# Attention plus gated MLP on one core: the second head pair is made the second unit of work, the tail the third, and the early loads are reordered

## The chip, the cores and the metric

The kernel runs on one core of a Trainium2 chip. The metric is device time in microseconds (us); the median of three runs of the kernel before is 283.36 us (282.83 to 284.4). The profiled execution has a span of 283.1 us. A difference of about 0.5% (1.4 us) is what a measurement of this kernel can tell from none.

## The reference

Two stages, for 8 batches, 8 heads, 576 tokens, head width 64, 128 features:

```python
def phi(x):
    proj = np.einsum('bhsd,df->bhsf', x, w_phi)
    proj = proj - np.max(np.abs(proj), axis=-1, keepdims=True)
    return np.concatenate([np.exp(proj), np.exp(-proj)], axis=-1)
q_p, k_p = (phi(q), phi(k))
kv = np.einsum('bhsf,bhsd->bhfd', k_p, v)
z = np.sum(k_p, axis=2)
num = np.einsum('bhsf,bhfd->bhsd', q_p, kv)
den = np.einsum('bhsf,bhf->bhs', q_p, z)[..., None] + 1e-06
x = (num / den)            # then (b, s, h*d)

h = np.maximum(x @ w_in, 0.0)
u, v = (h[..., :d_ff // 2], h[..., d_ff // 2:])
v_n = (v - mean(v)) / np.sqrt(var(v) + 1e-06)
v_s = np.einsum('ts,bsd->btd', w_spatial, v_n) + b_spatial[None, :, None]
out = (u * v_s) @ w_out
```

The first stage is linear attention with features exp(p) and exp(-p) of the projections p, scaled by their largest absolute value; the second is an MLP whose gate mixes tokens through `w_spatial`.

## The kernel before

**Units.** Of the 576 tokens of a batch, 512 are the main part (four blocks of 128) and 64 the tail. A *pair unit* is the main part of two heads of one batch (four per batch); a *tail unit* holds the tails of two batches, all heads. In the list `units`, the tail unit of a group of two batches stands ahead of that group, except for the first group, where it stands behind the first pair (lines 562 to 569). I call the four pairs of batch 0 p0 to p3. Before the change the order is p0, tail, p1, p2, p3, then the four pairs of batch 1, the next tail, batch 2 and so on.

**What a unit does.** `a_transpose` turns k and q (bf16 in SBUF) into kT and qT through TensorE and PSUM, with copies on VectorE. `a_keys` projects the keys (L256), takes the largest absolute value per token and head on VectorE (L268, `mk`), and the exponentials on ScalarE (L271, `kf`). `a_scale` computes the scale `em` on ScalarE (L291) and multiplies v with it on GpSimd (L296, `vs`; L298); for a tail unit `tail_scale` does this for one batch of the two (L311, `vst`; L313). `a_queries` takes the query maxima (L282) and splits them into two bf16 parts, `mhl`: on VectorE for the first five units, on GpSimd after that (L285, L286). `a_max_t` transposes `mhl` on TensorE (L317). `a_qfeat` makes the query features (L338 to L349, exponentials L355 on ScalarE). `a_kv` sums kf times vs, with the tail's part, over tokens (L368, L370); `a_num` multiplies by the query features and divides (L388); `a_x_t` transposes the result.

**The order of the work.** `step(i)` runs over the units as a software pipeline: in step i the keys and queries of unit i are done, the transposes of unit i+1 (`next`), and the later parts of earlier units by the lags in `LAGS`, `FIRST` and `FT`. Between them `fill` takes tasks of the MLP of a batch from a queue: `b_v` (L437), its ReLU (L439) and statistics (L440), `b_root` (L447 to L450 on GpSimd), `b_ln` (L454 on GpSimd, writes `vn`), `b_u` (L492), `b_s` (L513, reads `vn`), `b_o` (L538). Each engine takes its own instructions strictly in program order; what is wrapped in `pin` keeps its place, the rest may be moved by the framework's scheduler.

**Loads.** k and q are fp32 in memory and are cast to bf16 by the transfer itself; such transfers are issued by GpSimd (software queue, q0 in the profile). Transfers without a cast go through SyncE (hardware queue, q1). The loads of the head of the program: k and q of p0 as fp32 (`first`, cast on VectorE), v of batch 0 in one transfer of 1 MB and the tail's v through SyncE, and through GpSimd the tails of k and q, then k and q of p1, then of p2 and p3. The dictionary `io` holds what is issued behind a given step: the loads of batch 1 and all weights at steps 1 to 4, and the loads of batch b from 6 steps ahead of its first unit. `weights_with_max` builds `wm`, which the units from batch 2 on need: 12 GpSimd instructions (L230 to L232), not pinned.

Buffers that two groups use in turn, `vst` (two tiles, zeros) and `vnt` (two tiles), are filled by ScalarE at the start.

Of the kernel before, what the change touches and what calls it, by code (L numbers as in the profile page):

```python
# [8 lines left out]
FP32 = mybir.dt.float32  # L9
BF16 = mybir.dt.bfloat16  # L10
AF = mybir.ActivationFunctionType
ALU = mybir.AluOpType
# [4 lines left out]
def kernel(  # L17
# [15 lines left out]
    nc = tc.nc  # L33

    B, H, S, D = q.shape
    F = w_phi.shape[1]
    DM = moe_w_in.shape[0]
    DFF = moe_w_in.shape[1]
    HALF = DFF // 2
    P = 128  # L40
    KC = DM // P
    NP = H // 2
    NB = 4
    T0 = NB * P
# [3 lines left out]
    DA = D + 2  # L48

    cpool = ctx.enter_context(tc.tile_pool(name="const", bufs=1))  # L50
# [4 lines left out]
    s2 = ctx.enter_context(tc.tile_pool(name="stage_b", bufs=2))  # L55
# [4 lines left out]
    def pin(start):  # L60
        return lambda *a, **kw: tc.keep_in_program_order(start(*a, **kw))

    def main_ap(t, b, h0=0, n=H):
        return bass.AP(tensor=t.tensor, offset=t.offset + (b * H + h0) * S * D,
                       ap=[[NB * D, P], [S * D, n], [1, NB * D]])
# [8 lines left out]
    XB = 2  # L74
# [14 lines left out]
    def half_tile(x, b, y):  # L89
        if b not in st:  # L90
            alloc(b)
        if st[b][x][y] is None:
            n = f"{x}_bf{(2 * b + y) % 4}"
            st[b][x][y] = ld.tile([P, 4, NB * D], BF16, tag=n, name=n, bufs=1)
        return st[b][x][y]

    def load(x, b, y, h0=0, n=4):
        t = half_tile(x, b, y)
        pin(nc.gpsimd.dma_start)(out=t[:, h0:h0 + n], in_=main_ap(q if x == "q" else k, b, 4 * y + h0, n))

    def load_v(b, y=None):
        if b not in st:
            alloc(b)
        h0, n = (0, H) if y is None else (4 * y, 4)
        pin(nc.sync.dma_start)(
            out=st[b]["v"][:, h0 * NB:(h0 + n) * NB, :].rearrange("p (h c) d -> p h (c d)", h=n),
            in_=main_ap(v, b, h0, n))

    def load_tail(x, g):
        if g not in gs:  # L110
            alloc_tail(g)
        t, eng = dict(q=(q, nc.gpsimd), k=(k, nc.gpsimd), v=(v, nc.sync))[x]
        for i in range(2):
            pin(eng.dma_start)(out=gs[g][x][i * TL:(i + 1) * TL], in_=tail_ap(t, 2 * g + i))

# [7 lines left out]
    wphi_f = cpool.tile([P, F], FP32)  # L123
# [1 line left out]
        nc.scalar.dma_start(out=wphi_f[i * D:(i + 1) * D, :], in_=w_phi)  # L125
    alloc(0)
    first = {}
    for x, t in (("k", k), ("q", q)):
        first[x] = s2.tile([P, 2, NB * D], FP32, tag="ob", name="first", bufs=6)
        pin(nc.sync.dma_start)(out=first[x], in_=main_ap(t, 0, 0, 2))  # L130
    ident = cpool.tile([P, P], BF16)
    make_identity(nc, ident)
    zero = cpool.tile([P, 1], BF16)
    pin(nc.vector.memset)(zero, 0.0)
    wphi2 = cpool.tile([P, 2 * F], BF16)
# [9 lines left out]
    for i in range(NM):  # L145
        for tiles, name in ((mhl, "mhl"), (mT, "mT")):
            t = cpool.tile([P, P], BF16, name=f"{name}{i}")
# [4 lines left out]
    wm = cpool.tile([P, H, F], BF16)  # L152
    sel1 = cpool.tile([P, H], BF16)
    sel = cpool.tile([P, H, F], BF16)
    pin(nc.vector.tensor_tensor)(out=sel1, in0=ident[:, 0:H], in1=ident[:, H:2 * H], op=ALU.add)
    pin(nc.vector.tensor_scalar)(out=sel, in0=sel1.unsqueeze(2).to_broadcast([P, H, F]), scalar1=-1.0,
                                 scalar2=None, op0=ALU.mult)
    for x in ("k", "q"):
        pin(nc.vector.tensor_copy)(out=half_tile(x, 0, 0)[:, 0:2], in_=first[x])
    vst, vnt = [], []  # L160
    for i in range(2):
        t = cpool.tile([P, 2, 2, H, DA], BF16, name=f"vst{i}")
        pin(nc.scalar.copy)(out=t.rearrange("p b s h d -> p (b s h d)"), in_=zero.to_broadcast([P, 4 * H * DA]))
        vst.append(t)
        if i == 0:
            for y in range(2):
                r = slice(y * D, (y + 1) * D)
                pin(nc.scalar.copy)(out=wphi2[r, y * F:(y + 1) * F], in_=wphi_f[r, :])
        t = cpool.tile([P, 2, HALF], BF16, name=f"vnt{i}")
        for bl, row in ((0, TL), (1, 0)):  # L170
            pin(nc.scalar.copy)(out=t[:, bl, :], in_=ident[:, row:row + 1].to_broadcast([P, HALF]))
        vnt.append(t)
    load_v(0)
    for x in ("k", "q", "v"):
        load_tail(x, 0)
    load("k", 0, 0, 2, 2)
    load("q", 0, 0, 2, 2)
    load("k", 0, 1)
    load("q", 0, 1)

    w_in_bf = cpool.tile([P, KC, DFF], BF16)
    w_out_bf = cpool.tile([P, KC, DM], BF16)
    wsp = s2.tile([P, NB, T0], BF16, tag="vn", name="wsp", bufs=2)
# [41 lines left out]
    def merged(u):  # L225
        return u["pair"] and u["b"] >= XB

    def weights_with_max():
        for j in range(0, H, 2):
            nc.gpsimd.tensor_copy(out=wm[:, j, :], in_=wphi2[:, 0:F])  # L230
            nc.gpsimd.tensor_tensor(out=wm[:, j + 1, :], in0=wphi2[:, F:2 * F], in1=sel[:, j + 1, :], op=ALU.add)
            nc.gpsimd.tensor_copy(out=wm[D:D + 2 * H, j, :], in_=sel[0:2 * H, j, :])  # L232

    def q_even(u):
        u["qE"] = qts[u["i"] % len(qts)]
# [52 lines left out]
    def a_scale(u):  # L288
        em = small.tile([P, 2, H], FP32, tag="em" if u["pair"] else "em_t", name="em", bufs=3 if u["pair"] else 1)
        for s, sc in ((0, -1.0), (1, 1.0)):  # L290
            nc.scalar.activation(out=em[:, s, :], in_=u["mk"], func=AF.Exp, bias=0.0, scale=sc)  # L291
        if u["pair"]:
            pj = u["pj"]
            vs = feat.tile([P, 2, H, DA], BF16, tag="vs", name="vs", bufs=4)
            for s in range(2):
                nc.gpsimd.tensor_tensor(out=vs[:, s, :, 0:D], in0=st[u["b"]]["v"][:, pj * H:(pj + 1) * H, :],  # L296
                                        in1=em[:, s, :].unsqueeze(2).to_broadcast([P, H, D]), op=ALU.mult)
            nc.gpsimd.tensor_copy(out=vs[:, :, :, D:DA], in_=em.unsqueeze(3).to_broadcast([P, 2, H, 2]))  # L298
            u["vs"] = vs
        else:  # L300
            d = gs[u["g"]]
            d["vs"], d["unit"], d["em"] = vst[u["g"] % 2], u, em
            for bl in range(2 if u["i"] > 1 else 1):
                tail_scale(u["g"], bl)

    def tail_scale(g, bl):
        d = gs[g]
        vs, em = d["vs"], d["em"]
        r = slice(bl * TL, (bl + 1) * TL)
        for s in range(2):  # L310
            nc.gpsimd.tensor_tensor(out=vs[r, bl, s, :, 0:D], in0=d["v"][r],  # L311
                                    in1=em[r, s, :].unsqueeze(2).to_broadcast([TL, H, D]), op=ALU.mult)
        nc.gpsimd.tensor_copy(out=vs[r, bl, :, :, D:D + 1].rearrange("p i n o -> p i (n o)"), in_=em[r])  # L313

    def a_max_t(u):
        pt = psum.tile([P, P], BF16, tag="bank", name="pt")
# [240 lines left out]
    for g in range(G):  # L557
        if g > 0:
            units.append(dict(pair=False, g=g, i=len(units)))
        for b in (2 * g, 2 * g + 1):  # L560
            for pj in range(NP):
                units.append(dict(pair=True, g=g, b=b, pj=pj, i=len(units)))
                if b == 0 and pj == 0:
                    units.append(dict(pair=False, g=g, i=len(units)))
    NU = len(units)

# [36 lines left out]
    CAP = 2.11  # L603
    LAGS = dict(next=-1, maxima=1, features=2, sums=2, attention=3, out=4)
    FIRST = dict(next=-1, maxima=1, features=2, sums=2, attention=3, out=3)
    credit = [0.0]

    def fill(share):
# [6 lines left out]
    FT = dict(next=-1, maxima=1, features=2)  # L615

    def lag(u, what):
        return (FT if u["i"] == 1 else FIRST if u["pair"] and u["b"] == 0 else LAGS).get(what, 0)

    lists = [u["i"] + lag(u, "out") for u in units if u["pair"] and u["pj"] == NP - 1]  # L620

# [42 lines left out]
    def at(i, f, *a):  # L664
        io.setdefault(i, []).append(lambda: f(*a))

    at(1, load, "k", 1, 0)
    at(1, load, "q", 1, 0)
    at(1, load, "k", 1, 1)
    at(1, load, "q", 1, 1)  # L670
    at(1, load_v, 1)
    at(2, load_weight, w_in_bf[:, :, HALF:DFF], cols[:, :, HALF:DFF])
    at(3, load_weight, wsp, rows[:, :, 0:T0])
    at(3, load_weight, wspr, rows[:, :, T0:S])
    at(3, load_weight, wspt, moe_w_spatial[T0:S, :])
    at(4, tail_scale, 0, 1)
    at(4, load_weight, w_in_bf[:, :, 0:HALF], cols[:, :, 0:HALF])
    at(4, load_weight, w_out_bf, moe_w_out.rearrange("(kc p) f -> p kc f", p=P))
    for u in units:
        i = u["i"]  # L680
        if not u["pair"] and u["g"] > 0:
            early = 1 if u["g"] > 1 else 0
            at(i - AT - early, load_tail, "k", u["g"])
            for x in ("q", "v"):
                at(i - AT + 1 - early, load_tail, x, u["g"])
        if u["pair"] and u["b"] >= XB:
            if u["pj"] == 0:
                for n, (x, y) in enumerate((("k", 0), ("q", 0), ("k", 1), ("q", 1))):
                    at(i - AB + n, load, x, u["b"], y)
                for y in range(2):  # L690
                    at(i - AB + 1 + 2 * y, load_v, u["b"], y)
            for x in ("k", "q"):
                at(i - XP, cross, x, u)
    at(7, weights_with_max)
    for u in units:
        if merged(u):
            at(u["i"] - 1, q_even, u)
# [36 lines left out]
```

## Time and profile before

| what | value |
|---|---|
| time, median | 283.36 us |
| TensorE matmul busy | 256.1 us, 90% of the span |
| VectorE, ScalarE, GpSimd busy | 229.9, 223.2, 198.6 us |
| 10 to 15 us: TensorE, VectorE, ScalarE, GpSimd busy | 0.58, 0.81, 1.91, 2.99 us of 5 |
| 35 to 40 us: the same | 4.53, 5.00, 4.86, 5.00 us of 5 |
| 80 to 90 us: the same | 9.89, 9.65, 9.02, 7.78 us of 10 |
| HBM read, written | 32.85 MB, 9.44 MB |

How to read it: the shares over the whole span hide three stages. In the first 20 us TensorE has little to do, since data come in; from there to about 65 us all of VectorE, ScalarE and GpSimd are near full; after that TensorE is near full to the end. A change to the head of the program is worth what it moves at the entry of the last stage, not what it saves at the head.

### The profile page before, as it was taken

Reading aid. Unit: us, or ns where it says so; the run is one execution under the profiler, and the core shown is the slowest. Engines: PE = TensorE matmul, PEld = TensorE weight load, DVE = VectorE, ACT = ScalarE, POOL = GpSimd, SP = SyncE. Lnnn points to the kernel's source line nnn. Section 1 sums busy time; section 2 is a strip of 40 time slices with the busy share of each in tenths; the row PEclk is TensorE's granted clock in tenths of the full one; section 3 lists DMA queues with packets and bytes.
Section 4 is the critical chain, followed back from the end, with each engine's and each line's share of the span. In section 5 each row is a group of like instructions: output and inputs, shape, how many; then the busy total and the mean of one; then the engine's idle time right before and its main releaser. Section 6 shows DMA issues by size and latency. Waiting matters only on the chain.

```text
span 283.1 us, 8126 instructions
## 1 busy us (share of the span) xinstructions
PE 256.1 (90%) x3001; PEld 172.2 (61%) x3042; DVE 229.9 (81%) x575; ACT 223.2 (79%) x504; POOL 198.6 (70%) x358
## 2 busy tenths in 40 slices
PE   2267899989999999999999999999999999999993
PEld 1046686666766576666666676666765765654441
DVE  5279999987999988998889989997889897566441
ACT  7638999997899997899889987899789977723601
POOL 8549999999758995799949984889548832420710
PEclk9999999999999999999999999999999999999999
DMA  6977999999957999989999999999675301121205
GB/s 209 203 153 91 188 201 241 164 150 221 106 59 157 136 236 190 163 217 210 176 120 132 209 268 125 225 178 228 95 122 132 83 5 45 69 76 38 111 3 185
DMA packets 85100, 41.91 MB, mean 148 GB/s; under 512 B 52098, under 2 KB 80450, under 8 KB 85060
## 3 DMA queue, kind: packets, MB, share of 16 engines
q1 hardware_dynamic: 57348, 29.90, 51.5%
q0 software_dynamic: 27552, 11.41, 37.0%
q8 instruction: 24, 0.39, 0.6%
q14 instruction: 16, 0.13, 0.2%
q10 hardware_dynamic: 160, 0.07, 0.1%
HBM read 32.85 MB, written 9.44 MB: 149 GB/s over the span
## 4 chain that ended last, share of the span: by engine, by line
PE 63%; DVE 13%; ACT 11%; DMA 4%; POOL 3%; issue 3%; POOLq 0%; ACTq 0%; DVEq 0%
PE ps L513 9%; PE pv L437 9%; PE po L538 8%; PE pu L492 7%; PE ps L256 7%; PE pv L368 5%; ACT kf L271 5%; DMA q_tl<-in_q_dram 4%; PE pn L388 4%; DVE mk L268 3%; PE pq L334 3%; DVE stats L440 3%; PE ps L514 2%; ACT qf L355 2%; PE pn L416 2%
## 5 line engine op out<-in xcount | busy, mean ns | idle before, releaser
L271 ACT ACTIVATE kf<-ps 128x512 bf16<-128x512 f32 x144 | 76.1, 634 | 12.2 <-DVE mk L268 11.8
L296 POOL TENSOR_TENSOR vs<-v_f,em 128x512 bf16<-128x512 f32 x64 | 65.5, 1044 | 21.0 <-ACT em L291 19.5
L355 ACT ACTIVATE qf<-pq 128x512 bf16<-128x512 f32 x128 | 66.6, 619 | 9.0 <-PE pq L334 8.5
L268 DVE TENSOR_REDUCE mk<-ps 128x4 f32<-128x512 f32 x72 | 47.7, 678 | 0.9 <-issue 0.2
L282 DVE TENSOR_REDUCE mq<-ps 128x4 f32<-128x512 f32 x62 | 39.8, 681 | 2.5 <-PE ps L256 2.4
L513 PE MATMUL ps<-w_spT,vn 128*128 128x512 bf16 x116 | 32.4, 379 | 1.1 <-POOL vn L454 0.4
L440 DVE BATCH_NORM_STATS2 stats<-vr 128x6 f32<-128x512 bf16 (+1 forms) x40 | 26.7, 684 | 7.2 <-ACT vr L439 6.9
L516 DVE TENSOR_TENSOR uT<-ps,uT 128x512 bf16<-128x512 f32 x32 | 22.0, 687 | 12.9 <-PE ps L514 12.9
L538 PE MATMUL po<-w_out_bf,uT 128*128 128x512 bf16 x121 | 32.0, 379 | 0.4
L492 PE MATMUL pu<-xT,w_in_bf 128*128 128x512 bf16 x121 | 31.5, 379 | 0.5 <-issue 0.2
L437 PE MATMUL pv<-w_in_bf,xT 128*128 128x512 bf16 x116 | 30.7, 379 | 0.7
L439 ACT ACTIVATE vr<-pv 128x512 bf16<-128x512 f32 (+1 forms) x40 | 23.5, 615 | 7.3 <-PE pv L437 5.6
L368 PE MATMUL pv<-vs,kf 128*128 128x66 bf16 x512 | 24.5, 193 | 1.3 <-ACT kf L271 1.3
L379 DVE TENSOR_TENSOR x<-pn,rc 128x256 bf16<-128x256 f32 x64 | 24.9, 418 | 0.3
L454 POOL TENSOR_SCALAR vn<-vr,rs 128x512 bf16<-128x512 bf16 x32 | 24.3, 768 | 1.1
L388 PEld LDWEIGHTS <-qf 128*128 128x128 bf16 x512 | 20.2, 97 | 7.8 <-ACT qf L355 1.2
L368 PEld LDWEIGHTS <-kf 128*128 128x128 bf16 x512 | 21.9, 97 | 3.6 <-issue 2.6
L494 ACT ACTIVATE uT<-pu 128x512 bf16<-128x512 f32 x32 | 19.6, 639 | 4.9 <-PE pu L492 3.2
L388 PE MATMUL pn<-kv,qf 128*128 128x66 bf16 x512 | 21.9, 193 | 1.0 <-ACT qf L355 1.0
L541 ACT COPY ob<-po 128x512 f32<-128x512 f32 x18 | 11.0, 613 | 14.8 <-PE po L538 8.6
L311 POOL TENSOR_TENSOR vst<-v_tl,em 64x512 bf16<-64x512 f32 x16 | 16.3, 1038 | 8.6 <-ACT em L291 8.3
L370 PE MATMUL pv<-vst,kf 128*128 128x66 bf16 x128 | 21.2, 191 | 1.0 <-POOL vst L313 1.0
(128 smaller groups left out, 566.9 us busy)
## 6 DMA issues: line engine op xcount, KB each, us to landing
out_dram<-ob SPq DMA_DIRECT2D x32, 256.0 KB, 2.5
v_f<-in_v_dram SPq DMA_DIRECT2D x12, 512.0 KB, 5.9
k_bf<-in_k_dram POOLq DMA_DIRECT2D x15, 256.0 KB, 6.7
q_bf<-in_q_dram POOLq DMA_DIRECT2D x15, 256.0 KB, 7.5
v_f<-in_v_dram SPq DMA_DIRECT2D x2, 1024.0 KB, 11.7
qt<-qT_b SPq DMA_DIRECT2D x24, 64.0 KB, 4.8
v_tl<-in_v_dram SPq DMA_DIRECT2D x8, 128.0 KB, 5.2
w_in_bf<-in_moe_w_in_dram POOLq DMA_DIRECT2D x2, 512.0 KB, 8.3
```

The lines of the kernel that those rows point to most:

```text
L268: nc.vector.tensor_reduce(out=u["mk"][:, hs], in_=pk, axis=AX.X, op=ALU.max, apply_absolute_value=True)
L271: nc.scalar.activation(out=u["kf"][:, s, hs, :], in_=pk, func=AF.Exp, bias=0.0, scale=sc)
L282: nc.vector.tensor_reduce(out=mq[:, 4 * half:4 * half + 4], in_=pq, axis=AX.X, op=ALU.max, apply_absolute_value=True)
L296: nc.gpsimd.tensor_tensor(out=vs[:, s, :, 0:D], in0=st[u["b"]]["v"][:, pj * H:(pj + 1) * H, :], in1=em[:, s, :].unsqueeze(2).to_broadcast( ...
L355: nc.scalar.activation(out=qf[:, s], in_=pq, func=AF.Exp, bias=0.0, scale=sc)
L368: nc.tensor.matmul(out=pv[:, hh, s, :], lhsT=u["kf"][:, s, 4 * hh + c, :], rhs=u["vs"][:, s, 4 * hh + c, :], start=(c == 0), stop=False)
L388: nc.tensor.matmul(out=pn[:, pos, :], lhsT=u["qf"][hh][:, s, pos, :], rhs=d["kv"][:, 2 * u["pj"] + hh, s, :], start=(s == 0), stop=(s == 1))
L437: nc.tensor.matmul(out=pv[r], lhsT=lhs(kc), rhs=w_in_bf[:, kc, HALF:DFF], start=(kc == 0), stop=(kc == KC - 1))
L440: nc.vector.bn_stats(out=stats[r], in_=dst[r])
L492: nc.tensor.matmul(out=pu, lhsT=w_in_bf[:, kc, dc * P:(dc + 1) * P], rhs=d["xT"][:, kc, :], start=(kc == 0), stop=(kc == KC - 1))
L513: nc.tensor.matmul(out=ps, lhsT=d["vn"][:, sp, cs], rhs=w_spT[:, sp, 0:T0], start=(sp == 0), stop=False)
L538: nc.tensor.matmul(out=po[r], lhsT=lhs(dc), rhs=w_out_bf[:, dc, :], start=(dc == 0), stop=(dc == KC - 1))
```

## The change

p1 becomes the second unit and the tail the third. So that p1 is there early, its k and q are loaded as fp32 too, by SyncE behind those of p0, and cast to bf16 by GpSimd. v of batch 0 comes in two halves (heads 0 to 3 and 4 to 7), now through GpSimd and behind the loads of k and q that are wanted sooner, as is the tail's v. ScalarE no longer fills the second `vst` (VectorE does, ahead of its first cast) and the second `vnt` (GpSimd does, behind step 1). The lags of the first two units grow (`HEAD`: sums 3, attention 4). Batch 1's first loads come behind step 0, batch 2's at steps 3, 3, 5 and 6; `w_in`'s first half at step 5, `w_spatial` at 4, `w_out` at 8; `weights_with_max` is pinned, in two halves, behind steps 6 and 7; `tail_scale` is pinned too, its second batch behind step 5. The purpose is to feed TensorE and ScalarE sooner at the start, where they wait for the tail's transfers.

```diff
-    for x, t in (("k", k), ("q", q)):
-        first[x] = s2.tile([P, 2, NB * D], FP32, tag="ob", name="first", bufs=6)
-        pin(nc.sync.dma_start)(out=first[x], in_=main_ap(t, 0, 0, 2))
+    for h0 in (0, 2):
+        for x, t in (("k", k), ("q", q)):
+            first[x, h0] = s2.tile([P, 2, NB * D], FP32, tag="ob", name="first", bufs=6)
+            pin(nc.sync.dma_start)(out=first[x, h0], in_=main_ap(t, 0, h0, 2))
...
+    pin(nc.vector.memset)(vst[1], 0.0)
...
-    load_v(0)
-    for x in ("k", "q", "v"):
-        load_tail(x, 0)
-    load("k", 0, 0, 2, 2)
-    load("q", 0, 0, 2, 2)
-    load("k", 0, 1)
-    load("q", 0, 1)
+    load_tail("k", 0)
+    load_tail("q", 0)
+    load("k", 0, 1, 0, 2)
+    load("q", 0, 1, 0, 2)
+    load_v(0, 0, nc.gpsimd)
+    for x in ("k", "q"):
+        pin(nc.gpsimd.tensor_copy)(out=half_tile(x, 0, 0)[:, 2:4], in_=first[x, 2])
+    load_tail("v", 0, nc.gpsimd)
+    load("k", 0, 1, 2, 2)
+    load("q", 0, 1, 2, 2)
+    load_v(0, 1, nc.gpsimd)
...
-                if b == 0 and pj == 0:
+                if b == 0 and pj == 1:
                     units.append(dict(pair=False, g=g, i=len(units)))
...
+    HEAD = dict(next=-1, maxima=1, features=2, sums=3, attention=4, out=4)
...
-    at(1, load, "k", 1, 0)
-    at(1, load, "q", 1, 0)
+    at(0, load, "k", 1, 0)
+    at(0, load, "q", 1, 0)
+    at(1, fill_vnt, 1, nc.gpsimd.tensor_copy)
...
-    at(3, load_weight, wsp, rows[:, :, 0:T0])
-    at(3, load_weight, wspr, rows[:, :, T0:S])
-    at(3, load_weight, wspt, moe_w_spatial[T0:S, :])
-    at(4, tail_scale, 0, 1)
-    at(4, load_weight, w_in_bf[:, :, 0:HALF], cols[:, :, 0:HALF])
-    at(4, load_weight, w_out_bf, moe_w_out.rearrange("(kc p) f -> p kc f", p=P))
+    at(4, load_weight, wsp, rows[:, :, 0:T0])
+    at(4, load_weight, wspr, rows[:, :, T0:S])
+    at(4, load_weight, wspt, moe_w_spatial[T0:S, :])
+    at(5, tail_scale, 0, 1)
+    at(5, load_weight, w_in_bf[:, :, 0:HALF], cols[:, :, 0:HALF])
+    at(8, load_weight, w_out_bf, moe_w_out.rearrange("(kc p) f -> p kc f", p=P))
...
-                    at(i - AB + n, load, x, u["b"], y)
+                    at((3, 3, 5, 6)[n] if u["b"] == XB else i - AB + n, load, x, u["b"], y)
...
-    at(7, weights_with_max)
+    at(6, weights_with_max, 0)
+    at(7, weights_with_max, 1)
```

More of the change, by code (lines that the diff above doesn't have):

```diff
@@ L99, in load, with load_v @@
         pin(nc.gpsimd.dma_start)(out=t[:, h0:h0 + n], in_=main_ap(q if x == "q" else k, b, 4 * y + h0, n))
-    def load_v(b, y=None):
+    def load_v(b, y=None, eng=nc.sync):
         if b not in st:
@@ L104, in load_v, with load_tail @@
         h0, n = (0, H) if y is None else (4 * y, 4)
-        pin(nc.sync.dma_start)(
+        pin(eng.dma_start)(
             out=st[b]["v"][:, h0 * NB:(h0 + n) * NB, :].rearrange("p (h c) d -> p h (c d)", h=n),
             in_=main_ap(v, b, h0, n))
-    def load_tail(x, g):
+    def load_tail(x, g, veng=nc.sync):
         if g not in gs:
             alloc_tail(g)
-        t, eng = dict(q=(q, nc.gpsimd), k=(k, nc.gpsimd), v=(v, nc.sync))[x]
+        t, eng = dict(q=(q, nc.gpsimd), k=(k, nc.gpsimd), v=(v, veng))[x]
         for i in range(2):
@@ L157, with fill_vnt @@
                                  scalar2=None, op0=ALU.mult)
+    vst = [cpool.tile([P, 2, 2, H, DA], BF16, name=f"vst{i}") for i in range(2)]
+    vnt = [cpool.tile([P, 2, HALF], BF16, name=f"vnt{i}") for i in range(2)]
+    pin(nc.vector.memset)(vst[1], 0.0)
     for x in ("k", "q"):
[L159 to L169, printed above, removed]
-        for bl, row in ((0, TL), (1, 0)):
-            pin(nc.scalar.copy)(out=t[:, bl, :], in_=ident[:, row:row + 1].to_broadcast([P, HALF]))
-        vnt.append(t)
-    load_v(0)
-    for x in ("k", "q", "v"):
-        load_tail(x, 0)
-    load("k", 0, 0, 2, 2)
-    load("q", 0, 0, 2, 2)
-    load("k", 0, 1)
-    load("q", 0, 1)
+        pin(nc.vector.tensor_copy)(out=half_tile(x, 0, 0)[:, 0:2], in_=first[x, 0])
+    def fill_vnt(i, copy):
+        for bl, row in ((0, TL), (1, 0)):
+            pin(copy)(out=vnt[i][:, bl, :], in_=ident[:, row:row + 1].to_broadcast([P, HALF]))
+    pin(nc.scalar.copy)(out=vst[0].rearrange("p b s h d -> p (b s h d)"), in_=zero.to_broadcast([P, 4 * H * DA]))
+    for y in range(2):
+        r = slice(y * D, (y + 1) * D)
+        pin(nc.scalar.copy)(out=wphi2[r, y * F:(y + 1) * F], in_=wphi_f[r, :])
+    fill_vnt(0, nc.scalar.copy)
+    load_tail("k", 0)
[9 more added lines that the diff above has]
+    load_v(0, 1, nc.gpsimd)
     w_in_bf = cpool.tile([P, KC, DFF], BF16)
@@ L226, in merged, with weights_with_max @@
         return u["pair"] and u["b"] >= XB
[L228 to L232, printed above, removed]
+    def weights_with_max(n):
+        for j in range(4 * n, 4 * n + 4, 2):
+            pin(nc.gpsimd.tensor_copy)(out=wm[:, j, :], in_=wphi2[:, 0:F])
+            pin(nc.gpsimd.tensor_tensor)(out=wm[:, j + 1, :], in0=wphi2[:, F:2 * F], in1=sel[:, j + 1, :], op=ALU.add)
+            pin(nc.gpsimd.tensor_copy)(out=wm[D:D + 2 * H, j, :], in_=sel[0:2 * H, j, :])
     def q_even(u):
@@ L302, in a_scale @@
             d["vs"], d["unit"], d["em"] = vst[u["g"] % 2], u, em
-            for bl in range(2 if u["i"] > 1 else 1):
+            for bl in range(2 if u["g"] else 1):
                 tail_scale(u["g"], bl)
@@ L310, in tail_scale @@
         for s in range(2):
-            nc.gpsimd.tensor_tensor(out=vs[r, bl, s, :, 0:D], in0=d["v"][r],
+            pin(nc.gpsimd.tensor_tensor)(out=vs[r, bl, s, :, 0:D], in0=d["v"][r],
                                     in1=em[r, s, :].unsqueeze(2).to_broadcast([TL, H, D]), op=ALU.mult)
-        nc.gpsimd.tensor_copy(out=vs[r, bl, :, :, D:D + 1].rearrange("p i n o -> p i (n o)"), in_=em[r])
+        pin(nc.gpsimd.tensor_copy)(out=vs[r, bl, :, :, D:D + 1].rearrange("p i n o -> p i (n o)"), in_=em[r])
     def a_max_t(u):
@@ L617, in lag @@
     def lag(u, what):
-        return (FT if u["i"] == 1 else FIRST if u["pair"] and u["b"] == 0 else LAGS).get(what, 0)
+        if u["i"] < 5:
+            return (HEAD if u["i"] < 2 else FIRST if u["pair"] else FT).get(what, 0)
+        return LAGS.get(what, 0)
     lists = [u["i"] + lag(u, "out") for u in units if u["pair"] and u["pj"] == NP - 1]
```

## The prediction

> **What bounds the kernel now.** I read the slices of the page first, then the waits of the first 40 us, then GpSimd's instructions in order of time to 75 us beside TensorE's.
>
> ```profile
> ## 2 busy tenths in 40 slices
> PE   2267899989999999999999999999999999999993
> ...
> POOL 8549999999758995799949984889548832420710
> ...
> DMA  6977999999957999989999999999675301121205
> ...
> PE pt L249 <- DMA k_tl<-in_k_dram: 5.5, 1, 5.5
> ...
> PE pt L249 <- DMA q_tl<-in_q_dram: 2.2, 1, 2.2
> ```
>
> A slice is 7.1 us. TensorE starves in the first three slices (waits 5.5 + 2.2 us for the tail's k and q), climbs while GpSimd stands at 9 from the fourth slice to the tenth, and is full from there. GpSimd's rows show that full stretch in detail:
>
> ```profile
> 11.89 2.04 POOL L296 TENSOR_TENSOR vs<-v_f,em 128x512 bf16<-128x512 f32 x2 [2.90 <-ACT em L291]
> ...
> 20.37 2.04 POOL L311 TENSOR_TENSOR vst<-v_tl,em 64x512 bf16<-64x512 f32 x2 [3.39 <-ACT em L291]
> ...
> 45.99 0.20 POOL L286 TENSOR_TENSOR mhl<-mq,mhl 128x8 bf16<-128x8 f32 x1
> ...
> 63.74 0.25 POOL L447 TENSOR_SCALAR var<-mv 128x4 f32<-128x4 f32 x1
> ...
> 67.50 2.26 POOL L454 TENSOR_SCALAR vn<-vr,rs 128x512 bf16<-128x512 bf16 x3
> ...
> 73.84 2.05 POOL L296 TENSOR_TENSOR vs<-v_f,em 128x512 bf16<-128x512 f32 x2 [0.55 <-ACT em L291]
> ```
>
> The bracket is the idle time ahead of a row. After 20.37 none has one until 73.84: GpSimd is behind with its work for 53 us. TensorE's rows show who feels that:
>
> ```profile
> 47.47 0.23 PE L317 MATMUL pt<-ident,mhl 128*128 128x128 bf16 x1
> ...
> 71.61 1.03 PE L513 MATMUL ps<-w_spT,vn 128*128 128x512 bf16 x3
> ```
>
> The second batch-1 unit's `mhl` is ready at 46.2 and used at 47.47: 1.3 us to spare. Batch 0's last `vn` is ready at 67.50 + 2.26 = 69.8; L513 starts at 71.61 and takes that fourth block as its fourth matmul, at about 72.3: 2.5 us to spare. So GpSimd is nearly the bound at the entry of the full TensorE stage, though no long wait names it. After 72 us TensorE is 99% busy, so a shift there stays to the end.
>
> **What the skill says.** *DMA: Bandwidth & Descriptors*, Queues, rings and completion order: each DMA engine takes turns packet by packet between the queues it has work for. The trace agrees: in 5 to 10 us q1 moved 1662 packets and q0, which began later, 1277. Same page, Latency and other measured facts: two of the sixteen DMA engines are usually slower, with software descriptors as a guessed cause. The trace has no engine numbers, but landings lag the bulk of the traffic as one slow engine would make them (below). *GPSIMD Engine Reference*, 3.1: a one-input body takes 1.03 to 1.8 cycles of 1.2 GHz an element, 0.44 to 0.77 us for 512; the trace's one-input `vn` took 0.77.
>
> **The change, part by part.**
>
> *Removed at the head.* ScalarE loses one `vst` fill (1.95 us) and one `vnt` fill (1.13 us), so p0's kf, at 9.67 before, starts when `mk` is there, near 7.5. TensorE's wait for k_tl goes: p1 fills it. p1's kf (2.06) moves from 21.5 to near 10.5. The tail's q still lands near 14.5 to 16 (16.2 before), so kf of the tail stays near 16 to 18 and ScalarE is one kf ahead, some 2 to 5 us, if nothing else holds the pipeline. VectorE's added clear of `vst` (about 1.0 us, from 0.54 for 576 words of `w_spT` to 1056 words) lies in its 1.11 us wait for the first k.
>
> *Added on GpSimd, hidden.* Until about 12 us it idles anyway for v: two casts of 128x512, 0.44 to 1.04 us each (page's low price; the L296 row as the high), take 0.8; four more transfers issued (0.75 each, as L61's rows).
>
> *When can the first vs (L296) start?* This is the unknown; I call it T0, 11.89 before. It needs em (kf near 7.5 to 9.6, em 9.9) and v's first half, which now stands in the software queue behind both tails (2048 packets of 256 B read) and p2's k and q (512 packets of 1 KB), and is 512 packets itself; SyncE's queue has 1024 packets of k and q, and then, since v of batch 0 no longer stands there, at once the 1024 of batch 1's v. That is 3072 large and 2048 small packets. In 15 to 18.4 us some 1200 mostly large ones moved: 350 a us; 10 to 15 us (1377 large, 1051 small) then gives some 980 a us for small ones. 3072/350 + 2048/980 = 8.8 + 2.1 = 10.9 us, from the first packets at 2.5 us: 13.4, with completion near 14. That is the low end. But a load lands with its slowest engine: batch 0's v in the kernel before was the 1536th large packet of its queue, due at 2.5 + 1536/350 = 6.9, and landed at 1.75 + 9.8 = 11.55. And the k half-load behind the tails (issued 4.66, 13.2 to landing) landed at 17.9 after a like amount of traffic. High end 18 to 19. I take 17.4: 13.4 plus most of that 4.65 us lag.
>
> *GpSimd from T0 on.* The changed program's order on GpSimd gives, up to `b_root` of batch 0: 8 pair vs at 2.13 = 17.0; two `tail_scale` of group 0 at 2.15 = 4.3; group 1's two, 4.6; 9 k/q loads at 0.77 = 6.9; 4 tail loads, 2.85; `w_in` twice, `w_out`, `w_spatial`: 4.6; four `mhl` at 0.5 = 2.0 and the tail's 0.55; `wm` 4.3; the `vnt` fill, 2 x 0.6 to 0.77 = 1.4; batch 0's tail normalisation 2.4. Sum 51 us. Before, the same span is 63.74 - 11.89 = 51.85 with 3.39 idle, 48.5 of work: the change adds the `vnt` fill (1.4) and about 1.3 of `wm` that lay ahead of the first vs. What it really loses is the idle time that hid `wm` at the head. It is never idle after T0: each em it needs comes first by my timeline. So `b_root` starts at 17.4 + 51.0 = 68.4 against 63.74, and the last `vn` is ready 6.0 later (69.76 - 63.74), at 74.4.
>
> *What that does to TensorE.* The second batch-1 unit's `mhl` ends at T0 + 31.5 = 48.9 against a use at 47.47: +1.4 us. Then the fourth matmul of the first L513 group, at 72.3 before, waits for 74.4: **+2.1 us**. TensorE is in order, so everything behind it waits too. Later uses have 5 us or more (vs of batch 2's first pair ready 73.1, used 79.36), so GpSimd's lag of 4.7 goes no deeper. The head's gain is eaten: the sums of p0 now wait for the tail's `vst`, at T0 + 10.8 = 28.2 (22.6 before), and with them the last matmul of p1's query features, scheduled behind them.
>
> *At nothing:* later `w_out` (near 57, first used by batch 0's outputs in batch 1's list, after 80), later `w_spatial` (near 35, used at 57), sooner batch 2 loads (no wait for k or q of batch 2 before). Issues of the second half of the head loads wait for landings of the tails' transfers (their completion semaphores are reused after eight transfers); T0 waits longer anyway.
>
> So 283.36 + 2.1 = 285.5.
>
> **The rivals.** *A, v lands early (T0 13.5 to 15.5).* For it: the traffic count. `vn` is ready at T0 + 57 = 70.5 to 72.5, so -1.8 to +0.2: about 282.6 (no measurable change to slightly faster). Against it: the landing lags in the kernel before.
> *B, GpSimd isn't binding, and the head's gain reaches the end.* For it: no wait of over 1.0 us on GpSimd before; the fills that move off ScalarE. The gain is the one kf plus fill time that ScalarE gets ahead, some 3 us: 280.4. Against it: GpSimd without a gap from 20 to 73 us, and 3 us more work there.
> *C, deeper loss.* v near 19.5, GpSimd slowed by VectorE's copies, or TensorE waiting for vs as well: T0 + 57 - 72.3 = +4.2, 287.6.
>
> **The numbers.** Forecast (+1.0 to +3.3) 0.45, A 0.25, B 0.14, C 0.16. Range 281.0 to 288.0: some of B below it and some of C above. Faster by over 0.5% (under 281.9): B and a quarter of A, 0.20. Slower by over 0.5% (over 284.8): C and most of the forecast, 0.53. The same: 0.27.
>
> **What would show it.** Right: the first L296 near 17, held by the transfer of v; GpSimd without idle from there to past 70 us; its first L447 for a whole batch (now L452) near 68; TensorE idle for one to two us ahead of L513 (now L518), put down to GpSimd's `vn`; ScalarE busy near 10 to 12 us, then a hole near 23 to 28 us that ends with `vst`. Wrong: the first vs at 14 or sooner, or no TensorE wait on GpSimd between 45 and 75 us; then batch 2 starts ahead of 61.7 and the kernel is faster. If GpSimd has gaps after T0, my sum of its work is too high or it waits for others, and the loss is elsewhere.

## The result

The changed kernel takes **287.18 us** (median of four runs, 286.56 to 287.75) against 283.31 us for the kernel before (four runs, 282.83 to 284.4): a ratio of 1.0131 with a 95% interval of 1.0095 to 1.0167. It is slower; the forecast was 285.5. A second measurement (below) gave 286.85 against 284.79, ratio 1.0063 (1.0032 to 1.0093). All ratios are those on record; some lie up to 0.0025 below the quotient of the two medians beside them. The profiled execution has a span of 285.8 us.

### The profile after

The slices of the page of the changed kernel:

```profile
## 2 busy tenths in 40 slices
PE   3491998989899999999999999999999999999993
...
POOL 8569999999987995699957994789558842420710
```

TensorE is fed sooner (9 in the third slice, 6 before), then falls to 1 in the fourth (7 before). That hole, from 21 to 28 us, undoes the gain: before, TensorE waited 5.55 and 2.21 us for the tail's k and q and 1.01 for the tail's `vst`; now it waits 3.09 for the q and 6.32 for the `vst`. GpSimd's rows say what it waited for (start, duration, engine, line, operation; the bracket is the idle time ahead of the row and what ended it):

```profile
17.03 2.04 POOL L301 TENSOR_TENSOR vs<-v_f,em 128x512 bf16<-128x512 f32 x2 [2.59 <-DMA v_f<-in_v_dram]
...
25.54 2.06 POOL L61 TENSOR_TENSOR vst<-v_tl,em 64x512 bf16<-64x512 f32 x2
...
48.71 0.20 POOL L291 TENSOR_TENSOR mhl<-mq,mhl 128x8 bf16<-128x8 f32 x1
...
68.67 0.25 POOL L452 TENSOR_SCALAR var<-mv 128x4 f32<-128x4 f32 x1
...
72.43 2.27 POOL L459 TENSOR_SCALAR vn<-vr,rs 128x512 bf16<-128x512 bf16 x3
```

The first `vs` starts at 17.03, held by the transfer of v (11.89 before, held by `em`). From there to 72.43 only one row of GpSimd (not among these) has a bracket, 0.44 us. TensorE's rows show who pays:

```profile
27.84 0.21 PE L375 MATMUL pv<-vst,kf 128*128 128x66 bf16 x1 [6.32 <-POOL vst L61]
...
48.97 0.23 PE L322 MATMUL pt<-ident,mhl 128*128 128x128 bf16 x1 [0.41 <-POOL mhl L291]
...
74.00 0.39 PE L518 MATMUL ps<-w_spT,vn 128*128 128x512 bf16 x1 [0.37 <-POOL vn L459]
...
74.75 0.39 PE L518 MATMUL ps<-w_spT,vn 128*128 128x512 bf16 x1 [0.36 <-POOL vn L459]
```

Before, the same group of four (L513) ran in 1.03 us from 71.61 on, so that its fourth matmul began 0.64 later (one alone takes 0.39), at 72.25. Now its third and fourth come 0.75 us apart, the pace of `vn` (0.76 us each), and the fourth stands at 74.75: 2.5 us later. No wait in this group is over 0.37 us, yet the fourth matmul is late by 2.5: a bound that shows as two short brackets. Part of this TensorE had lost before: the group begins at 72.92, 1.3 us later than before, and unbroken it would have put its fourth matmul at 73.56. The rest, 1.2 us, is the hold by `vn`.

### The profile page after: what moved, and what is told of

It is laid out like the page before. It is cut to its first block, busy times and chain, and to the rows that moved or that the text cites. A ratio compares the mean times of both kernels' runs of the same rounds, so it can differ in the third digit from the quotient of the medians.

```text
span 285.8 us, 8175 instructions
## 1 busy us (share of the span) xinstructions
PE 260.5 (91%) x3042; PEld 174.8 (61%) x3042; DVE 230.6 (81%) x576; ACT 220.6 (77%) x501; POOL 203.6 (71%) x366
## 4 chain that ended last, share of the span: by engine, by line
PE 61%; POOL 17%; DVE 7%; DMA 5%; ACT 5%; issue 3%; POOLq 0%; ACTq 0%; DVEq 0%
PE ps L518 9%; PE pv L442 9%; PE po L543 9%; PE ps L261 7%; PE pu L497 6%; PE pv L373 5%; PE pn L393 4%; DMA v_f<-in_v_dram 4%; POOL vs L301 4%; PE pq L339 3%; PE ps L519 2%; POOL vst L61 2%; ACT kf L276 2%; DVE stats L445 2%; POOL vn L459 2%
## 5 line engine op out<-in xcount | busy, mean ns | idle before, releaser
L518 PE MATMUL ps<-w_spT,vn 128*128 128x512 bf16 x128 | 33.7, 379 | 1.4 <-POOL vn L459 1.4
L497 PE MATMUL pu<-xT,w_in_bf 128*128 128x512 bf16 x128 | 32.1, 379 | 0.0
L442 PE MATMUL pv<-w_in_bf,xT 128*128 128x512 bf16 x128 | 31.5, 379 | 0.1
L373 PEld LDWEIGHTS <-kf 128*128 128x128 bf16 x512 | 22.6, 99 | 8.9 <-issue 7.9
L375 PE MATMUL pv<-vst,kf 128*128 128x66 bf16 x128 | 21.8, 194 | 6.3 <-POOL vst L61 6.3
L373 PE MATMUL pv<-vs,kf 128*128 128x66 bf16 x512 | 25.3, 196 | 1.3 <-ACT kf L276 1.3
L61 POOL TENSOR_TENSOR vst<-v_tl,em 64x512 bf16<-64x512 f32 x16 | 16.4, 1041 | 5.3 <-ACT em L296 4.9
```

The lines of the kernel that those rows point to most:

```text
L373: nc.tensor.matmul(out=pv[:, hh, s, :], lhsT=u["kf"][:, s, 4 * hh + c, :], rhs=u["vs"][:, s, 4 * hh + c, :], start=(c == 0), stop=False)
L442: nc.tensor.matmul(out=pv[r], lhsT=lhs(kc), rhs=w_in_bf[:, kc, HALF:DFF], start=(kc == 0), stop=(kc == KC - 1))
L497: nc.tensor.matmul(out=pu, lhsT=w_in_bf[:, kc, dc * P:(dc + 1) * P], rhs=d["xT"][:, kc, :], start=(kc == 0), stop=(kc == KC - 1))
L518: nc.tensor.matmul(out=ps, lhsT=d["vn"][:, sp, cs], rhs=w_spT[:, sp, 0:T0], start=(sp == 0), stop=False)
```

## The experiments

From each profile I take T0 (the start of the first `vs`), the moment when the last `vn` of batch 0 is ready, and the start of the fourth matmul of the first L513 group (L518 in the changed kernel; L514 or L517 where lines have moved), which reads it and with which TensorE enters its full stage. Where a group runs unbroken its fourth matmul begins 0.64 us after its start.

| kernel | T0 | last `vn` ready | fourth matmul | span | span less fourth |
|---|---|---|---|---|---|
| before | 11.89 | 69.76 | 72.25 | 283.1 | 210.85 |
| before, second profile | 13.17 | 70.74 | 73.37 | 284.3 | 210.9 |
| changed | 17.03 | 74.70 | 74.75 | 285.8 | 211.05 |
| changed, second profile | 15.59 | 73.25 | 73.31 | 284.3 | 211.0 |
| changed, `wm` late | 16.38 | 70.29 | 72.92 | 284.2 | 211.3 |
| changed, v first | 10.54 | 70.14 | 70.19 | 280.9 | 210.7 |
| changed, batch 1 loads later | 16.29 | 73.34 | 73.39 | 284.4 | 211.0 |
| changed, three fills | 16.15 | 75.36 | 75.41 | 286.4 | 211.0 |
| changed, five fills | 16.20 | 77.64 | 77.70 | 289.0 | 211.3 |
| before, `wm` pinned as after | 11.89 | 73.55 | 73.61 | 284.3 | 210.7 |
| before, `wm` late | 14.03 | 69.61 | 72.06 | 283.6 | 211.5 |
| before, v late | 15.13 | 70.83 | 71.90 | 282.6 | 210.7 |
| v first, `wm` late | 12.13 | 67.97 | 70.57 | 282.1 | 211.5 |
| v first, loads later | 11.24 | 68.24 | 70.89 | 282.1 | 211.2 |

The last column is 210.7 to 211.5 in all 14: what the head does to the time, it has done, to within 0.8 us, when that matmul starts.

### `wm` behind step 11

```diff
-    at(6, weights_with_max, 0)
-    at(7, weights_with_max, 1)
+    at(11, weights_with_max, 0)
+    at(11, weights_with_max, 1)
```

> Changed kernel with weights_with_max behind step 11 in place of steps 6 and 7. Backlog theory (the entry of the full TensorE stage is set by GpSimd's work behind the first vs): 4.3 us of GpSimd work leave the stretch ahead of batch 0's vn, the last vn is ready near 70.4 instead of 74.7 and no longer awaited; what stays is the 1.5 us that TensorE is late at the mhl of the second batch-1 unit (49.0 against 47.5). About 1 us faster than the changed kernel: 286.2, or 284.8 if all but the 1.5 us goes. Head theory (the loss is TensorE's wait for the tail's vst at 21 to 28 us with its lower clock, and lasts from there): no change, 287.2.

Measured: 286.12 us, ratio 1.0061 (1.0042 to 1.008): 0.7 to 1.1 us under the changed kernel's two medians. As ratios the gain is clear against the first measurement (1.0131) and none against the second (1.0063); the trace says more. `vn` came 4.4 us sooner than in the changed kernel's first profile, and the whole group ran unbroken. TensorE's row:

```profile
72.28 1.03 PE L518 MATMUL ps<-w_spT,vn 128*128 128x512 bf16 x4
```

The waits on `vn` are gone, and the fourth matmul comes 1.8 us sooner, not 4.4: behind GpSimd's `vn` stands TensorE's own late head as the next bound (it still waits 6.99 us for `vst`, and 0.73 for `mhl`).

### v ahead of the tails

```diff
             pin(nc.sync.dma_start)(out=first[x, h0], in_=main_ap(t, 0, h0, 2))
+    load_v(0, 0)
...
-    load_v(0, 0, nc.gpsimd)
...
-    load_v(0, 1, nc.gpsimd)
...
+    at(0, load_v, 0, 1, nc.gpsimd)
```

> Changed kernel with the first half of batch 0's v loaded by SyncE right behind k and q of the first two pairs, and the second half issued by GpSimd behind step 0. Backlog theory: the first vs starts near 11 instead of 17.0, all of GpSimd follows 5 to 6 us sooner until other engines bind; the last vn near 69, TensorE 3 to 4 us ahead of the kernel before: about 279.8. If the tails of k and q land later through it (15 to 16 instead of 13.4), ahead by only 1.5 to 2: 281.5. Theory that the moved weight and batch 2 loads cost the time: no change, 287.2.

Measured: 284.04 us, ratio 0.9993 (0.9974 to 1.0011); this profile is of the fastest of its runs (282.73). T0 fell by 6.5 us, the fourth matmul by 4.6, since GpSimd now idles 1.25 us for an `em` and 0.37 for a transfer. So v's place costs the changed kernel 2 to 4 us (ratios 1.0063 and 1.0131 against 0.9993), but with it undone the new order is no better than the old one; the 279.8 to 281.5 expected did not come. `vn` still holds two matmuls:

```profile
69.44 0.39 PE L517 MATMUL ps<-w_spT,vn 128*128 128x512 bf16 x1 [0.36 <-POOL vn L458]
70.19 0.39 PE L517 MATMUL ps<-w_spT,vn 128*128 128x512 bf16 x1 [0.36 <-POOL vn L458]
```

### Batch 1's k and q behind step 2

```diff
-    at(0, load, "k", 1, 0)
-    at(0, load, "q", 1, 0)
-    at(1, load, "k", 1, 1)
-    at(1, load, "q", 1, 1)
+    for y in range(2):
+        at(2, load, "k", 1, y)
+        at(2, load, "q", 1, y)
```

> Changed kernel with batch 1's k and q loads issued behind step 2 instead of 0 and 1, so that GpSimd does the tail's vst 3.0 us sooner with the same work up to vn. Backlog theory: TensorE's 6.3 us wait shrinks to about 3.3, but mhl and vn come when they did: 287.2, within 0.5. Head theory: 3 us faster, 284.2.

Measured: 286.34 us, ratio 1.0082 (1.0052 to 1.0112); against the changed kernel 0.8 us less than its first median and 0.5 less than its second. `vst` starts at 21.72 in place of 25.54 and TensorE resumes at 24.00 in place of 27.84:

```profile
24.00 0.21 PE L375 MATMUL pv<-vst,kf 128*128 128x66 bf16 x1 [5.17 <-POOL vst L61]
...
47.65 0.23 PE L322 MATMUL pt<-ident,mhl 128*128 128x128 bf16 x1 [1.34 <-POOL mhl L291]
...
73.39 0.39 PE L518 MATMUL ps<-w_spT,vn 128*128 128x512 bf16 x1 [0.36 <-POOL vn L459]
```

Of these 3.8 us the fourth matmul keeps 1.36, of which the sooner T0 alone accounts for 0.74. The head theory, which wanted 3 us, fails: TensorE, early, waits 1.34 us for `mhl` and then for `vn` again, since GpSimd's work is the same and only its order has changed.

### The kernel before with `wm` pinned behind steps 6 and 7

```diff
-    at(7, weights_with_max)
+    at(6, weights_with_max, 0)
+    at(7, weights_with_max, 1)
```

> Kernel before with one part of the change: weights_with_max pinned behind steps 6 and 7, so that it no longer lies in GpSimd's idle time at the head. Backlog theory: 4.3 us more GpSimd work between the first vs and vn, last vn at 69.8 + 4.3 = 74.1 against TensorE's need at 72.3: 1.8 us slower than before, 285.1. Head theory and load theory: no change, 283.3.

Measured: 285.47 us, ratio 1.0054 (1.0033 to 1.0076). Nothing is changed but the place of `wm`, whose 12 instructions are now pinned in two halves. GpSimd's idle time ahead of the first `vs` grows from 2.90 to 4.46 us, and ahead of the first `vst` from 3.39 to 5.69: 3.9 us in which `wm` had cost nothing. The last `vn` is now ready 3.8 us later (73.55, not 69.76):

```profile
11.89 2.04 POOL L296 TENSOR_TENSOR vs<-v_f,em 128x512 bf16<-128x512 f32 x2 [4.46 <-ACT em L291]
...
19.79 2.04 POOL L311 TENSOR_TENSOR vst<-v_tl,em 64x512 bf16<-64x512 f32 x2 [5.69 <-ACT em L291]
...
71.28 2.27 POOL L454 TENSOR_SCALAR vn<-vr,rs 128x512 bf16<-128x512 bf16 x3
```

TensorE's row of the fourth matmul then has the changed kernel's bracket:

```profile
73.61 0.39 PE L513 MATMUL ps<-w_spT,vn 128*128 128x512 bf16 x1 [0.36 <-POOL vn L454]
```

In this profile TensorE's clock is halved for a while near 22 to 25 us, which the first profile of the kernel before doesn't have there. That is not what makes the runs slower: where the mean granted clock is 0.999 or more, the median is 285.4 us here (eight runs) and 284.0 in the kernel before beside it (37 runs).

### More work on GpSimd

The second `vnt` is filled three times, and five times, with the same values. This is the edit for three; for five, four lines are added.

```diff
     at(1, fill_vnt, 1, nc.gpsimd.tensor_copy)
+    at(1, fill_vnt, 1, nc.gpsimd.tensor_copy)
+    at(1, fill_vnt, 1, nc.gpsimd.tensor_copy)
```

> The changed kernel with its second vnt filled three times in place of once, all behind step 1: four more GpSimd instructions of 0.58 us, 2.3 us in all, with the same values. Backlog theory: GpSimd has no idle time between the first vs and the last vn of batch 0, so b_root and vn come 2.3 us later and TensorE enters its full stage 2.3 us later: the ratio to the kernel before rises from 1.013 to 1.021. Rival (the late vst and the slower clock at the head set the time, GpSimd only trails): ratio stays at 1.013.

> The changed kernel with its second vnt filled five times in place of once: eight more GpSimd instructions of 0.60 us, 4.8 us in all, with the same values. Three fills (2.4 us more) had moved the last vn by 1.5 us counted from the first vs, since 0.4 us of GpSimd's idle time went first. Backlog theory: 4.8 less some 0.6 us, 4 us later: ratio to the kernel before 1.014 above that of the changed kernel beside it. Rival (TensorE is held by others too, GpSimd's share of it is small): less than 2 us more, under 0.007.

Measured: three fills 289.33 us, ratio 1.0158 (1.0128 to 1.0187), under the 1.021 expected; its interval overlaps the first one of the changed kernel and decides nothing alone; in its trace `vn` came 59.2 us after T0 (57.7 in the changed kernel). Five fills, beside the changed kernel: 290.81 against 286.85 us, ratios 1.0198 (1.0173 to 1.0223) and 1.0063: 4.0 us more. GpSimd's fills, then TensorE's row:

```profile
22.04 5.62 POOL L61 COPY vnt<-ident 128x512 bf16<-128x512 bf16 x10
```

```profile
77.70 0.39 PE L518 MATMUL ps<-w_spT,vn 128*128 128x512 bf16 x1 [0.36 <-POOL vn L459]
```

The ten copies take 5.62 us where the changed kernel's two take 1.17: 4.45 us of added work, of which 0.44 can go into the idle time that GpSimd had. The rest, 4.0 us, comes out at the end of the program (3.8 in the trace at the fourth matmul, counted from T0).

### The kernel before with `wm` late

```diff
-    at(7, weights_with_max)
+    at(11, weights_with_max, 0)
+    at(11, weights_with_max, 1)
```

> The kernel before with its wm moved behind step 11 in two pinned halves. Slack theory of the prediction: its vn was ready 2.5 us ahead of its use and its mhl 1.3 us, so GpSimd binds nothing there: ratio 1.000, within 0.3%. Rival (GpSimd's load in the 20 to 65 us stretch slows the pipeline even where no wait names it): 1 to 2 us faster, ratio 0.994.

Measured: 284.94 us, ratio 1.0023 (1.0001 to 1.0045). No gain, as the slack theory says. Of the small loss of 0.8 us the trace names 0.28, which TensorE waits for the late `wm`:

```profile
81.11 0.23 PE L334 MATMUL pq<-qt,wm 128*128 128x128 bf16 x1 [0.28 <-POOL wm L61]
```

T0 was 14.03 here, 2.1 us later than in the first profile, and the fourth matmul no later.

### The kernel before with v late

```diff
...
-    load_v(0)
     for x in ("k", "q", "v"):
         load_tail(x, 0)
     load("k", 0, 0, 2, 2)
     load("q", 0, 0, 2, 2)
+    load_v(0, 0, nc.gpsimd)
     load("k", 0, 1)
     load("q", 0, 1)
+    load_v(0, 1, nc.gpsimd)
```

> The kernel before with one part of the change alone: batch 0's v goes out in two halves on GpSimd's software queue, the first behind the tails and the second pair's k and q, the other behind the third and fourth pair's; the order of units and all else stay. The first vs then starts near 16 to 17 in place of 11.9. Sum theory (vn is ready at T0 plus GpSimd's work, which here is some 54.5 to 55.5 us without the idle time that the late v replaces, against 57.7 in the changed kernel): vn ready at 70.5 to 72.5, used at 72.3: no loss or a few tenths, ratio 1.000 to 1.003. Rival (a late v by itself is the loss): 2 us or more, ratio 1.008 or higher.

Measured: 284.42 us against 284.79, ratio 0.9975 (0.9958 to 0.9991). A late v by itself is not the loss; if anything it is a small gain, less than the 0.5% that a measurement of this kernel can tell. In its trace TensorE has the tail's q at 12.0 (16.4 before), and `vst` follows `vs` at once:

```profile
15.13 2.04 POOL L297 TENSOR_TENSOR vs<-v_f,em 128x512 bf16<-128x512 f32 x2 [5.91 <-DMA v_f<-in_v_dram]
17.31 2.03 POOL L312 TENSOR_TENSOR vst<-v_tl,em 64x512 bf16<-64x512 f32 x2
```

In the old order `vst` is GpSimd's second multiply, and the idle time for `em` ahead of it (3.39 us before, none here) absorbs the delay. In the new one it comes after two pairs' `vs`, the `vnt` fill and four transfer issues, with no idle time among them.

### Both kernels once more

> The kernel before once more, for a second look. The profile on record took 284.9 us, 1.5 above the median of its own runs (283.36), and I put the shift read in it on top of the median. If that profiled execution was late at the head, this one has a span of 281.5 to 282.5, with the fourth matmul of the first L513 group 0.8 to 1.5 us sooner than 72.3. Rival: the fourth L513 matmul stands at 72.3 again within 0.3 us, and the executions differ behind it.

> The changed kernel again, beside the kernel before on one chip. My prediction put a shift read from one profile on the median. If the profiled execution of the kernel before was a late one (284.9 us against a median of 283.4), the ratio here is again 1.010 to 1.014, while the fourth L518 matmul stands within 0.5 us of 74.75 less what the first vs starts sooner than 17.03. Rival (the later part of the program is slower after the change too): that matmul as said, but more than 211.5 us from it to the end of the span.

Measured: the kernel before, 286.13 us (one run, span 284.3), its fourth matmul at 73.37, later and not sooner than in the first profile: neither expectation held. T0 is 1.3 us later there, but `vn` is ready 2.6 us ahead of the fourth matmul, and the tail's q is no later (TensorE resumes with it at 16.19; 16.36 in the first profile). What differs is TensorE's pace: from 22.5 to 25.8 us its granted clock reads 0.50, in the first profile 1.00. First the rows of the first profile, then those of the second:

```profile
22.69 0.29 PE L368 MATMUL pv<-vs,kf 128*128 128x66 bf16 x4
...
26.36 0.39 PE L388 MATMUL pn<-kv,qf 128*128 128x66 bf16 x7 [0.26 <-ACT qf L355]
```

```profile
22.52 0.41 PE L368 MATMUL pv<-vs,kf 128*128 128x66 bf16 x4
...
27.39 0.39 PE L388 MATMUL pn<-kv,qf 128*128 128x66 bf16 x7 [0.15 <-ACT qf L355]
```

Across this stretch the second profile goes from 0.17 us ahead to 1.03 behind, and at the fourth matmul it is 1.12 behind. The other runs of the kernel before fit: those with a mean granted clock of 0.990 or lower (13) have a median of 285.1 us, the other 88 one of 284.1.

The changed kernel: 286.85 us against 284.79, ratio 1.0063 (1.0032 to 1.0093), below the 1.010 to 1.014 that I expected; the place of the fourth matmul came as expected. Its GpSimd row:

```profile
15.59 2.04 POOL L301 TENSOR_TENSOR vs<-v_f,em 128x512 bf16<-128x512 f32 x2 [2.71 <-DMA v_f<-in_v_dram]
```

And TensorE's:

```profile
73.31 0.39 PE L518 MATMUL ps<-w_spT,vn 128*128 128x512 bf16 x1 [0.36 <-POOL vn L459]
```

T0 and the fourth matmul are both 1.44 us sooner than in the first profile: in the changed kernel the matmul follows T0 after 57.7 us both times.

### Versions meant to gain

v ahead, and `wm` behind step 11 (the two edits above together):

> The changed kernel with both of my reliefs for GpSimd at once: batch 0's first half of v on the hardware queue right behind the four fp32 loads, and the 4.3 us of wm behind step 11. Backlog theory (TensorE enters its full stage when GpSimd's last vn of batch 0 is ready): with v first alone that vn was ready at 70.1 and still held L517 twice by 0.36 us; without wm it comes near 65.9 and holds nothing, as the late wm alone brought 1.6 us of span. So a span near 280, about 1.5 us less than with v first alone: ratio to the kernel before 0.994. Rival (TensorE, VectorE and ScalarE are near full from 30 to 65 us on their own account, and GpSimd's relief buys nothing once v is early): as v first alone, ratio 0.999.

Measured: 283.99 us against 284.12, ratio 0.9991 (0.9971 to 1.0011). The backlog theory fails here: `vn` is ready at 67.97, 2.6 us before its use, and nothing is won. TensorE's row:

```profile
69.93 1.03 PE L517 MATMUL ps<-w_spT,vn 128*128 128x512 bf16 x4
```

With GpSimd relieved, TensorE comes to this point no sooner; it waited 3.49 us for `vst` and 0.67 for `mhl` on the way, and in this profile its clock is halved from 24.4 to 27.7 us, which it is not there with v first alone. Which of these holds it stays open.

v ahead, batch 1's loads behind step 2, and `wm` behind step 10:

> The changed kernel with v of batch 0 first on the hardware queue, batch 1's k and q loads behind step 2 (so that vst of the tail comes ahead of four transfer issues on GpSimd), and wm behind step 10, in place of 11, where the first unit of batch 2 waited 0.28 us for it. If the wait of TensorE for vst (3.49 us with v first and wm late) is what keeps that version from gaining, vst comes 2 to 3 us sooner and the fourth L517 matmul 1 to 1.5 us: ratio to the kernel before 0.995 or lower, a span near 280.5. Rival (from 30 to 65 us VectorE, ScalarE and GpSimd together set the pace, and what the head saves is waited for there): 0.999, as without the moved loads.

Measured: 283.31 us against 284.79 for the kernel before, ratio **0.9949** (0.9924 to 0.9975): faster than the kernel before by about the 0.5% that a measurement can tell, and clearly faster than the changed kernel (286.85 in the same measurement). GpSimd's row, then TensorE's:

```profile
19.03 2.03 POOL L61 TENSOR_TENSOR vst<-v_tl,em 64x512 bf16<-64x512 f32 x2 [1.51 <-ACT em L295]
```

```profile
21.32 0.19 PE L374 MATMUL pv<-vst,kf 128*128 128x66 bf16 x1 [1.17 <-POOL vst L61]
...
44.92 0.23 PE L321 MATMUL pt<-ident,mhl 128*128 128x128 bf16 x1 [2.05 <-POOL mhl L290]
```

`vst` waits for its `em` now and no longer for GpSimd, but TensorE, early, loses 2.05 us to `mhl`, which stands behind other work on GpSimd. Two edits changed at once against the version before it, and the profiles' fourth matmuls (70.89 and 70.57) don't show the gain: the ratio came as expected, the sooner fourth matmul that was to bring it did not. What brought it stays open.

## Why the prediction was right, and where it was off

- **T0.** Predicted 17.4, held by v: 17.03, and from 15.59 to 16.38 in the five other profiles with that head. The first agrees, and it is the latest of the six; the others are some 1 us sooner. That the first came within 0.4 us is in part luck: the 17.4 was 13.4 from a count of packets plus "most of" a lag seen once, and no run shows what causes that lag. The count alone, 13.4, was not seen.
- **GpSimd's work.** Predicted 51.0 us from T0 to `b_root`; measured 68.67 - 17.03 = 51.6, with 0.44 of it idle. Ahead of T0, in idle time, the two casts took 0.64 and 0.61 us (0.8 for both predicted). The `vnt` fill took 1.17 (1.4 predicted). The last `vn`: 74.4 predicted, 74.70.
- **TensorE.** +1.4 at `mhl`: from 47.47 to 48.97, +1.5. +2.1 at the fourth matmul: +2.5. Nothing was given back or lost behind it (210.85 and 211.05 to the end). Two readings were off. The prediction had TensorE idle for one to two us at this group; it idles 0.73 in two brackets, since it arrives 1.3 us late itself. And "99% busy after 72 us" holds from 70 to 90 us; from 90 to 100 it is 92%.
- **Head.** ScalarE's hole, predicted from 23 to 28, is 5.96 us up to 29.02, and ends with a matmul (L347) that stood behind the one waiting for `vst` (TensorE resumes with `vst` at 27.84; 28.2 predicted).
- **Which part of the loss is whose.** The prediction had GpSimd losing the idle time that hid `wm` at the head. Shown: `wm` in the full stretch costs the old kernel a ratio of 1.0054 by itself, and v late costs it nothing. In the profiles T0 came 5.1 us later and `vn` 4.9; the slack of 2.5 (72.25 - 69.76) was used up first, and 2.5 remain. GpSimd's late start and its lost idle time together make the bound that holds. The next bound is 1.2 us behind it: TensorE's own late head, at 73.56. With `wm` moved away that bound is what is left: 72.92, with T0 0.65 sooner.
- **The size.** The forecast was 1.7 us short of 287.18. The term that was mis-sized is the base; the mechanism held: "283.36 + 2.1" puts a shift read in one execution on a median. The profiled execution of the kernel before had taken 284.9 us, 1.5 over that median; 284.9 + 2.5 = 287.4, against 287.75 for the profiled execution after. By the table's last column (an estimate; the span is some 1.8 us less than the time) a run of 283.31 us has its fourth matmul near 70.6, one of 284.79 near 72.1. The 72.3 of the prediction fits the second measurement and is 1.7 late for the first. The two differences of medians, 3.9 and 2.1 us, belong to ratios whose intervals don't meet: the second falls on the forecast of +2.1, the first beyond its band (+1.0 to +3.3), where the prediction had put rival C, though C's causes (v near 19.5, slower GpSimd work, a wait for `vs`) are not in the profile. That the loss is between 2 and 4 us is as much as these runs settle.
- **Not foreseen: another slow spell of TensorE, behind the hole.** Its rows for the same projection (L261, four matmuls) after the change:

```profile
19.15 0.60 PE L261 MATMUL ps<-wphi,qt 128*128 128x256 bf16 x4
...
28.89 1.06 PE L261 MATMUL ps<-wphi,kT 128*128 128x256 bf16 x4
...
35.09 0.60 PE L261 MATMUL ps<-wphi,qt 128*128 128x256 bf16 x4
```

  0.60 us, 1.06 behind the hole, 0.60 again; the granted clock reads 0.50 from 25.9 to 32.7 us. In the first profile of the kernel before the four take 1.06 to 0.83 us up to 20.69 and 0.61 from 24.77 on. Its page gives the clock as full in the slow part too, so the durations tell more than the clock's row. The Trainium skill (*TensorE: Matmul & The Clock Gate*, Part 1) says that an idle window of some 3.4 us halves the clock until TensorE has been busy for about as long. Here the halving agrees, 4.5 us after TensorE fell idle and until 4.8 us after it resumed. The 3.4 us are not borne out as a limit to plan by: in the second profile of the kernel before the clock fell at 22.5 us, and in the 6 us ahead of that no wait of TensorE was longer than 1.24. The spell costs the end little as long as the end waits for GpSimd, whose only idle time after T0, 0.44 us for an `em` at 32.59, bounds what it can have lost to this. What the spell adds to TensorE's own late head was not tried by itself.
- **Rivals.** A (v early, T0 from 13.5 to 15.5, no loss) fell with T0; 15.59 in the second profile stands at its edge, and the kernel was slower there too. B (the head's gain reaches the end) fell with the moved loads: 3.8 us sooner at the hole, 1.36 at the entry. C's +4.2 at the fourth matmul was not reached in the profile (+2.5).
- **A reading that shows less than it says.** The packets that the prediction counts for the two queues in 5 to 10 us (1662 and 1277) show that both were served in the same stretch, not that they took turns.

## What to carry to other kernels

When an engine runs without idle time up to where the full stage begins, and the first work of that stage waits for it, the entry comes at its start plus its work. Price a reordering by how it moves that start and by the idle time it takes away, even if the waits on that engine are short (0.37 us here). A relief is worth no more than the slack to the next bound: with v early, 4.3 us less of GpSimd work brought nothing. Before adding a shift to a median, see whether the profiled execution is itself at that median.

## What the runs showed of the hardware

- GpSimd held back transfers that it was due to issue: 1.36 us ahead of a q load and 1.14 ahead of v's second half, both until the tail's q had landed. In this program a late transfer so delayed the issue of later ones.
- The same head gave T0 from 15.59 to 17.03 in six profiles; the same loads of the kernel before let TensorE wait 5.55 + 2.21 us for the tail in one and 3.54 + 3.15 in another.
- The kernel before ran with and without a spell of halved clock at 22.5 to 25.8 us; with it the fourth matmul came 1.12 us later.
